# Split copies, half-batch loads and new ranks in the written-out order of an attention and FFN kernel

## The chip, the cores and the metric

The kernel runs on one core of one Trainium2 chip. The metric is the device time of one execution in microseconds. PE is the tensor engine, DVE the vector engine, ACT the scalar engine, POOL the GpSimd engine, which also issues most loads, and SP the sync engine.

## What is computed

Eight batches of eight heads, 576 positions and 64 dimensions go through a windowed attention. Heads 0 to 3 see the last 32 positions; heads 4 to 7 see every fourth of the last 128. The result, as 4608 rows of 512, goes through a multiplicative feed-forward network (FFN) without activation functions.

```python
scores = scale * np.matmul(q, k.transpose(0, 1, 3, 2))
mask_plain = (rel >= 0) & (rel < window)                                   # heads 0..3
mask_dil = (rel >= 0) & (rel < window * dilation) & (rel % dilation == 0)  # heads 4..7
attn = softmax(np.where(mask, scores, -1e9))
x = (attn @ v).transpose(0, 2, 1, 3).reshape(B * S, H * D)                 # 4608 x 512
a = x @ w1                                                                 # 512 -> 1024
b = x @ w2
h = a * b @ w3
out = h @ w_out                                                            # 1024 -> 512
```

## The kernel before

The kernel never forms `h @ w3`: it multiplies w3 by w_out once (1024 x 512, tile `wf_sb`) and applies the product to the gate `a * b`.

**Attention of a batch.** Heads come in two halves, u = 0 and u = 1. Loads bring q, k and v rows in bf16 (`load_rows`, line 245; for the u = 0 half of q and k of batch 0, whole float rows by `load_whole`, line 254, rounded by ACT in `round_rows`, line 271). DVE turns them with 32x32 transposes (`turn`, lines 379 and 394; the tasks are named T). PE forms scores in groups of blocks of 96 queries (line 445; tasks S). Batch 0 has four groups of three blocks, and a bias matmul (line 428) puts the mask into PSUM. Later batches have groups of five, and DVE multiplies by a mask after the exp (line 464; tasks M). ACT takes the exp (line 456; tasks E). In batches 0 and 1 the values are turned too: PE transposes them back (`v_back`, line 403; VT), and a copy puts them from PSUM into tile `vp` (`v_keep`, lines 413 and 415; VK). From batch 2 on values are loaded in place. For each quarter of a batch, PE multiplies by the values (line 481; V), DVE takes the reciprocal of the sums (line 492; R) and scales (line 504; N). In batches 0 and 1 PE transposes the result (line 521; X), and a copy puts it into tile `XT` (`keep`, lines 529 and 531; K). Later batches use a DMA transpose.

A task's name carries its place: K0.2 is the copy of batch 0, third quarter, and VK0.1.1 the value copy of batch 0, u = 1, second half.

**The FFN.** A unit is 288 rows, two to a batch. For unit k and column block f, PE forms A{k}.{f} and B{k}.{f} with four matmuls each (`up`, line 553), ACT copies A (line 564), and DVE multiplies both into the gate ring `gt` (line 569). The two units of batch 0 come first, four column blocks at a time in turn. The first product needs the copies K0.0, K0.1 and K0.2, and columns 0 to 255 of w1 and w2. Every 128 rows, eight matmuls with `wf_sb` make a piece of the output (`down`, line 580), which ACT copies and SP stores. w3 comes in eight blocks of rows: PE transposes one (line 638; W3T), ACT copies it (line 645; W3C), PE multiplies it by w_out (line 650; W3M), and ACT or DVE rounds it into `wf_sb` (lines 661 and 663; W3D).

**The order.** Every engine executes its instructions in a written-out order. `Plan.run` makes it when the kernel is built, as a list scheduler: each task has an engine, a duration in ns, dependencies and a priority; whenever an engine is free, the ready task with the lowest priority value goes next. The eight PSUM banks are places that matmul tasks hold (`slot`); while the first FFN product hasn't begun and PE has nothing, fillers (line 692) are put in. The priorities come from `FIRST` for batch 0 and `RANK` for the later ones. `ON_DVE` names the copies that DVE makes and not ACT. FFN products have running numbers from 10 as priorities, W3M has 7, and S, V, VT and X have values of about -99 plus the batch. The loads form one queue on POOL. Their order is that of the calls of `load`: the u halves of batch 0, then `FIRST_LOADS`. In that tuple "30" is the first block of w3, "w0" columns 0 to 255 of w1 and w2 (two loads), "w1" the next 256 and "w2" the last 512, "o0" and "o1" the halves of w_out, and "q1", "k1", "v1" the rows of batch 1. In the model a load takes its issue time on POOL and then its transfer time on one DMA line that all share.

Of the kernel before, what the change touches and what calls it, by code (L numbers as in the profile page):

```python
# [32 lines left out]
DIRECT_V = 2  # L33
ORDER = (2, 3, 0, 1)
RES = (0, 2, 1, 3)
RANK = dict(E=0.4, VK=2, K=0.3, N=1.5, T=3, VT=0.3, S=0.4, V=0.05, X=0.2, W=6, C=-1)
FIRST = {"E": 2, "VK": 0.4, "K": 0.5, "N": 0.2, "T": 2, "VT": 0.05, "S": 0.2, "V": 0.05, "X": 0.4}
WARM = 14
FILL = 110
FIRST_LOADS = ("30", "31", "w0", "w1", "32", "w2", "o0", "o1", "q1", "k1", "33", "34", "v1", "35", "36", "37")  # L40
SHIFT = {}
ON_DVE = ("VK0.0.1", "VK1.0.1", "W3D1", "W3D3", "W3D7")
GRP = 5
WHOLE = ("qn", "kn")
BUSY = 4500
LEAD = 1.1

# [12 lines left out]
class Plan:  # L60
# [13 lines left out]
        return t  # L74

    def run(self):
        fills = []
        users = {id(t): [] for t in self.tasks}
        takers = {id(t): [] for t in self.tasks}
        left = {}  # L80
# [38 lines left out]
        while len(order) < n:  # L119
            progress = True  # L120
            while progress:
                progress = False
                for e in engines:
                    if free[e] > now:
                        continue
                    for r, t in sorted(waiting[e], key=lambda x: x[1].prio):
                        if r > now:
                            continue
                        at = place(t) if t.slot else 0
                        if at is not None:  # L130
# [12 lines left out]
                    waiting[e].remove((r, t))  # L143
                    t.start = now
                    if e == "DMA":
                        free[e] = now + t.dur[0]
                        if t.dur[1]:
                            dma = max(dma, now + t.dur[0]) + t.dur[1]
                            t.end = dma + 1900
                        else:  # L150
                            t.end = free[e]
                    else:
                        t.end = free[e] = now + t.dur
                        if e == "SP" and t.name[0] == "X" and dma > now:
                            t.end = free[e] = now + t.dur + BUSY
                            dma += 1.5 * t.dur
                    if t.slot:
                        t.place = at
                        held[at : at + t.slot] = [t] * t.slot
                        if t.slot == 4:  # L160
                            kept = None
                    order.append(t)
                    for u in users[id(t)]:
                        left[id(u)] -= 1
                        if not left[id(u)]:
                            r = max(d.end + (0 if d.eng == u.eng else d.lat) for d in u.deps)
                            waiting[u.eng].append((r, u))
                    progress = True
# [11 lines left out]
def kernel(  # L180
# [46 lines left out]
    kts = [const.tile([P, 2, PADK + S, 2], BF16, name=f"kt{i}") for i in range(2)]  # L227
    qts = [const.tile([P, 2, S, 2], BF16, name=f"qt{i}") for i in range(2)]
    vts = [const.tile([P, 2, PADK + S, 2], BF16, name=f"vt{i}") for i in range(1)]
    warm = const.tile([P, 512], BF16, name="warm")  # L230

    def bank(n, dtype=F32):
        at = ps[:, plan.now.place or 0, :]
# [118 lines left out]
    def no_halo():  # L352
        nc.vector.memset(bias[0:32, 0:5:4, :], -BIG)

    def masks_of_bias():

        for at, first, n in ((0, 0, 4), (4, 1, 2), (6, 4, 3), (9, 4, 3), (12, 0, 4)):
            nc.gpsimd.tensor_scalar(
                out=mask[:, at : at + n, :],
                in0=bias[:, first : first + n, :],  # L360
                scalar1=0.0,
                scalar2=None,
                op0=AL.is_ge,
            )

# [39 lines left out]
                )  # L405
        spread[(b, u, half)] = x

    def v_keep(b, u, half, eng):
        dst = vps[b % 2][:, 4 * u : 4 * u + 4, 3 * half : 3 * half + 3, 0:D]
        o = dst.rearrange("p h m (j c) -> p m h j c", c=2)  # L410
        i = spread[(b, u, half)].rearrange("p m c (h j) -> p m h j c", h=4)
        if eng == "ACT":
            nc.scalar.copy(out=o, in_=i)
        else:
            nc.vector.tensor_copy(out=o, in_=i)
# [50 lines left out]
    class Step:  # L466
# [57 lines left out]
                    identity=ident[0:QB, 0:QB],  # L524
                )

        def keep(self, eng):
            if eng == "ACT":
                nc.scalar.copy(out=self.cols(), in_=self.x)
            else:  # L530
                nc.vector.tensor_copy(out=self.cols(), in_=self.x)

        def back_dma(self):
            nc.sync.dma_start_transpose(
# [12 lines left out]
            return XT[0][:, b * BLK : (b + 1) * BLK, c, 48 * hf : 48 * hf + 48]  # L547
        return XT[1][:, k, c - 2, :].rearrange("p (r m t) -> p m r t", r=2, m=BLK)

    def up(k, f, w_sb, key):  # L550
        o = bank(UNIT)
        for j, c in enumerate(ORDER):
            nc.tensor.matmul(  # L553
                out=o,
                lhsT=w_sb[:, c, f * P : (f + 1) * P],
                rhs=unit_cols(k, c),
                start=(j == 0),
                stop=(j == DCH - 1),
            )
        held[(key, k, f)] = o  # L560

    def copy_a(k, f):
        a_sb = wk_pool.tile([P, UNIT], BF16, tag="asb", bufs=6, name="asb")
# [106 lines left out]
        return (RANK if b else FIRST)[kind]  # L670

    def warm_up():
        o = bank(512)
        for i in range(WARM):
            nc.tensor.matmul(out=o, lhsT=warm[:, 0:P], rhs=warm, start=True, stop=True)

# [12 lines left out]
            nc.vector.memset(t[0:32, :, 0, 0:D], 0.0)  # L689

    def fill():
        nc.tensor.matmul(out=bank(256), lhsT=warm[:, 0:P], rhs=warm[:, 0:256], start=True, stop=True)  # L692

    plan.fill, plan.fill_from = fill, 2000

    c1 = add("const", "DVE", 1200, [], first_constants, -99)
    c0 = add("const2", "DVE", 1400, [c1], constants, -98)
    add("warm", "PE", 700 + 427 * WARM, [c1], warm_up, 0)

    lw3, lwo = {}, {}  # L700
    dma_n = [0]
# [41 lines left out]
            for half in range(2)  # L743
        ]
    plan.dma = 1200 + 1350 * len(WHOLE)
    for u in range(2):
        for nm in ("qn", "kn", "vn"):
            if u or nm not in WHOLE:
                loads_rows(nm, 0, (u,))
    idt = add("ident", "DMA", (600, 0), [], lambda: make_identity(nc, ident), 2.5, lat=150)  # L750
    bnd = add("band", "DMA", (800, 0), [c1], band, 1.5, lat=150)
    blk = add("blocks", "ACT", 1200, [bnd], blocks, -5, lat=100)
    blk = add("no halo", "DVE", 150, [blk], no_halo, 0, lat=80)
    mk = add("masks", "DMA", (2500, 0), [blk], masks_of_bias, 26.5, lat=150)
    lw12 = {}
    for x in FIRST_LOADS:
        c = int(x[1])
# [6 lines left out]
        elif x[0] == "v" and DIRECT_V <= c:  # L764
            loads_v(c)
        else:
            loads_rows(x[0] + "n", c)

    FUSED, w3m = [], []
    for ft in sorted(lw3):  # L770
# [10 lines left out]
        FUSED.append(add(name, eng, dur, [z], lambda f=ft, e=eng: w3_done(f, e), -1, lat=100))  # L781

    kept, paced = {}, []
    prev = {"x": [None] * 4}
    readers, grp_of, todo, n_grp, steps = {}, {}, [], 0, 0

    def turns(b, u, nm, pr):
# [22 lines left out]
    for b in range(B):  # L810
# [9 lines left out]
        for u in range(2):  # L820
# [3 lines left out]
            for half in range(2):  # L824
# [3 lines left out]
                if (b, u, half) == (0, 1, 1):  # L828
                    late.append(x)
                name = f"VK{b}.{u}.{half}"  # L830
                eng, dur = ("DVE", 980) if name in ON_DVE else ("ACT", 880)
                vals[(b, u, half)] = [
                    add(name, eng, dur, [x, c0], lambda b=b, u=u, h=half, e=eng: v_keep(b, u, h, e),
                        10 * b + rank("VK", b), lat=100)
                ]
        if b >= DIRECT_V:
            hal = add(f"HALO{b}", "DVE", 820, LV[b] + [c0], lambda b=b: halo_v(b), 10 * b + 2,
# [6 lines left out]
        def group(blocks, biased):  # L844
# [11 lines left out]
            else:  # L856
# [2 lines left out]
                e = add("E" + n, "ACT", 160 + 330 * g.n, [s], g.exps, 10 * b + rank("E", b), lat=100,  # L859
                        after=old)  # L860
                ms = [
                    add(f"M{n}.{h}", "DVE", 150 + 100 * g.n, [e, mk], lambda h=h: g.masks(h),
                        10 * b + 2, lat=80)
                    for h in range(2)
                ]
# [19 lines left out]
        while steps < 4 * B:  # L885
# [18 lines left out]
            rc = add(f"R{n}", "DVE", 240, [vv], st.recip, 10 * bb + rank("N", bb), lat=0,  # L904
                     after=[prev["x"][i]])
            ns = [
                add(f"N{n}", "DVE", 960 if u == 0 else 555, [vv, rc],
                    lambda st=st, part=part: st.norm(part), 10 * bb + rank("N", bb), lat=80)
# [2 lines left out]
            if bb < TURNED:  # L911
                x = add("X" + n, "PE", 310, ns + [idt], st.back, bb - 99 + rank("X", bb), slot=1)
                name = f"K{n}"
                eng, dur = ("DVE", 460) if name in ON_DVE else ("ACT", 640)
                x = add(name, eng, dur, [x], lambda st=st, eng=eng: st.keep(eng),
                        10 * bb + rank("K", bb), lat=100)
            else:
                x = add("XD" + n, "SP", 1300, ns, st.back_dma, 0, lat=1200)
            kept.setdefault(bb, []).append(x)
            prev["x"][i] = x  # L920
            vdone.setdefault(bb, []).append(vv)

    seq = 10
    G, Y, gates, stores, pairs = {}, {}, [], [], []

    def ups(k, f):
        nonlocal seq
        b, hf = k // 2, k % 2
        need = kept[b][0:2] + kept[b][2 + hf : 3 + hf]
# [3 lines left out]
        seq += 1  # L933
        a = add(f"A{k}.{f}", "PE", 490, need + wl, lambda: up(k, f, w1_sb, "a"), seq, slot=1,
                after=free + pairs[-1:])
        pairs.append(a)
        ca = add("CA", "ACT", 400, [a], lambda: copy_a(k, f), -1, lat=100,
                 after=[gates[-6] if len(gates) > 5 else None])
        seq += 1
        bb = add(f"B{k}.{f}", "PE", 490, need + wl, lambda: up(k, f, w2_sb, "b"), seq,  # L940
                 slot=1, after=[a])
        G[(k, f)] = add("G", "DVE", 460, [bb, ca], lambda: gate(k, f), -1, lat=100)
        gates.append(G[(k, f)])

    def downs(i):
# [71 lines left out]
```

## Time and profile before

| | before |
|---|---|
| time, three runs | 255.77, 255.88, 255.93 us |
| time of the profiled execution | 255.86 us |
| its span from first to last instruction | 254.1 us |
| PE, DVE, ACT, POOL busy | 246.2, 165.6, 125.9, 66.3 us |
| granted PE clock, mean | 1.000 |
| FFN products (L553) | 1024 matmuls, 136.2 us busy |
| second FFN step (L580) | 280 matmuls, 65.8 us busy |
| w3 times w_out (L650) | 64 matmuls, 14.8 us busy |
| fillers (L692) | 37 matmuls, 4.9 us busy |

PE's busy time counts a matmul from its start to its end, and matmuls overlap, so 0.286 us for a matmul of L553 is more than its share of the stream: in the chain of waits four of them take 0.49 us. Busy time of fillers is in the sum too.

Loads land in the order of issue, each some 6 to 19 us after it was issued:

| load | issued, us | landed, us |
|---|---|---|
| last half of v of batch 0 | 4.46 | 11.9 |
| w3 block 0 | 5.00 | 13.1 |
| w0, second of two | 6.8 | 17.3 |
| w1, second of two | 9.38 | 19.8 |
| w2, second of two | 13.37 | 26.4 |
| w_out, second half | 16.01 | 31.5 |
| q and k of batch 1 | 17.65, 18.77 | 35.0, 37.5 |
| v of batch 1 | 24.15 | 42.7 |
| w3 block 7 | 32.03 | 46.4 |

### The profile page before, as it was taken

What the parts mean: (1) busy time and instruction counts of PE and PEld (TensorE: products, weight loads), DVE (VectorE), ACT (ScalarE), POOL (GpSimd) and SP (SyncE); (2) the same over time, 40 slices, a digit from 0 to 9 for tenths busy, and PEclk for the clock granted to TensorE, in tenths of its full rate; (3) what the DMA queues carried; (4) which work ended last, traced back from release to release, by engine and by line L of the source; (5) the groups of instructions that cost most, each with busy time, mean ns of one, the idle gap of its engine ahead of it and who ended that gap; (6) DMA issues with size and microseconds to landing.
All of it is one profiled execution on the core that took longest, in us unless ns stands there. A gap on an engine that the chain in (4) does not pass through costs nothing.

```text
span 254.1 us, 6809 instructions
## 1 busy us (share of the span) xinstructions
PE 246.2 (97%) x2763; PEld 170.0 (67%) x2763; DVE 165.6 (65%) x342; ACT 125.9 (50%) x221; POOL 66.3 (26%) x103
## 2 busy tenths in 40 slices
PE   7699999999999999999999999999999999999994
PEld 3488766565777666667676766776767666777662
DVE  3983447799889898678767886837737365333321
ACT  5677333986635534463636626355353553333331
POOL 7653129643622712008260310700000000000000
PEclk9999999999999999999999999999999999999999
DMA  7999999999999999828999758852332223311114
GB/s 226 206 198 206 207 212 210 208 102 180 193 148 172 205 187 172 190 67 140 166 144 149 105 69 109 121 100 67 65 67 67 66 68 67 101 33 56 42 41 124
DMA packets 59374, 33.40 MB, mean 131 GB/s; under 512 B 44752, under 2 KB 49232, under 8 KB 59344
## 3 DMA queue, kind: packets, MB, share of 16 engines
q0 software_dynamic: 38544, 18.81, 58.0%
q1 hardware_dynamic: 20656, 14.10, 24.8%
q8 instruction: 21, 0.34, 0.6%
q14 instruction: 9, 0.07, 0.1%
q10 hardware_dynamic: 144, 0.07, 0.1%
HBM read 38.80 MB, written 9.44 MB: 190 GB/s over the span
## 4 chain that ended last, share of the span: by engine, by line
PE 93%; ACT 3%; DMA 2%; DVE 1%; issue 0%; ACTq 0%
PE ps L553 50%; PE ps L580 24%; PE ps L650 5%; PE ps L481 4%; PE ps L445 4%; DMA gt<-in_q_dram 2%; ACT et L456 2%; PE ps L692 2%; PE ps L638 1%; PE ps L403 1%; PE ps L521 1%; ACT w3T L645 1%; PE ps L598 1%; DVE qt L394 1%; ACT qn L271 0%; DVE kt L379 0%
## 5 line engine op out<-in xcount | busy, mean ns | idle before, releaser
L553 PE MATMUL ps<-XT,w_sb 128*128 128x288 bf16 x1024 | 136.2, 286 | 0.0
L553 PEld LDWEIGHTS <-w_sb 128*128 128x128 bf16 x1024 | 97.8, 98 | 30.6
L569 DVE TENSOR_TENSOR gt<-ps,asb 128x288 bf16<-128x288 f32 x128 | 57.7, 455 | 51.9 <-PE ps L553 49.6
L564 ACT CAST asb<-ps 128x288 bf16<-128x288 f32 x128 | 50.8, 398 | 51.9 <-PE ps L553 49.6
L580 PE MATMUL ps<-wf_sb,gt 128*128 128x512 bf16 x280 | 65.8, 379 | 0.0
L591 ACT COPY osb<-ps 128x512 f32<-128x512 f32 x35 | 20.5, 585 | 56.4 <-PE ps L580 54.6
L580 PEld LDWEIGHTS <-gt 128*128 128x128 bf16 x280 | 27.4, 98 | 26.9
L293 POOL DMA_DIRECT2D vp<-in_v_dram x48 | 29.9, 630 | 40.7 <-PE ps L481 18.5
L456 ACT ACTIVATE et<-ps 128x1920 bf16<-128x1920 f32 (+2 forms) x21 | 34.2, 1633 | 5.5 <-PE ps L445 4.8
L504 DVE TENSOR_TENSOR xo<-ps,rcp 96x384 bf16<-96x384 f32 (+1 forms) x48 | 31.5, 676 | 0.6
L464 DVE TENSOR_TENSOR et<-et,mask 128x960 bf16<-128x960 bf16 (+1 forms) x34 | 21.4, 645 | 4.9 <-ACT et L456 4.7
L394 DVE STREAM_TRANSPOSE qt<-qn 128x320 uint32<-128x320 uint32 (+3 forms) x34 | 22.4, 669 | 2.1 <-ACT qn L271 1.9
L481 PEld LDWEIGHTS <-et 128*128 128x128 bf16 x384 | 14.3, 98 | 1.7
L481 PE MATMUL ps<-vp,et 128*128 128x65 bf16 x384 | 15.1, 193 | 0.0
L650 PE MATMUL ps<-wo_sb,w3T 128*128 128x512 bf16 x64 | 14.8, 379 | 0.1
L394 DVE STREAM_TRANSPOSE kt<-kn 128x320 uint32<-128x320 uint32 (+3 forms) x18 | 11.6, 644 | 4.4 <-PE ps L445 4.3
L445 PE MATMUL ps<-qt,kt 32*128 32x96 bf16 x768 | 12.1, 201 | 1.9 <-DVE kt L379 1.9
L445 PEld LDWEIGHTS <-kt 32*128 32x128 bf16 x768 | 9.1, 92 | 7.0 <-issue 4.5
L492 DVE RECIPROCAL rcp<-ps 96x12 f32<-96x12 f32 x32 | 6.8, 216 | 10.6 <-PE ps L481 10.3
L245 POOL DMA_DIRECT2D kn<-in_k_dram x8 | 5.5, 685 | 27.9 <-DVE kt L394 16.2
L379 DVE STREAM_TRANSPOSE kt<-kn 128x576 uint32<-128x576 uint32 (+1 forms) x9 | 9.9, 1121 | 1.4 <-PE ps L445 1.4
L650 PEld LDWEIGHTS <-w3T 128*128 128x128 bf16 x64 | 5.9, 98 | 6.8 <-ACT w3T L645 0.6
(55 smaller groups left out, 118.2 us busy)
## 6 DMA issues: line engine op xcount, KB each, us to landing
qn<-in_q_dram POOLq DMA_DIRECT2D x7, 576.0 KB, 8.1
kn<-in_k_dram POOLq DMA_DIRECT2D x7, 576.0 KB, 7.4
w3n<-in_moe_w_dram POOLq DMA_DIRECT2D x8, 256.0 KB, 15.2
out_dram<-osb SPq DMA_DIRECT2D x7, 256.0 KB, 2.5
out_dram<-osb SPq DMA_DIRECT2D x8, 224.0 KB, 3.0
vp<-in_v_dram POOLq DMA_DIRECT2D x6, 288.0 KB, 10.3
out_dram<-osb SPq DMA_DIRECT2D x8, 192.0 KB, 2.9
out_dram<-osb SPq DMA_DIRECT2D x8, 160.0 KB, 3.9
```

Of the source, the lines that this page charges most:

```text
L293: nc.gpsimd.dma_start(out=vp[32 + p0 : 32 + p0 + n, 4:8, m, 0:D], in_=v_rows(b, 4, 4 * t0 + res, [[4 * D, n], [S * D, 4], [1, D]]),)
L394: nc.vector.transpose(out=o, in_=i)
L445: nc.tensor.matmul(out=self.sp[:, g, QB * i : QB * i + QB], lhsT=kt[prt, u, QB * m : QB * m + P, c], rhs=qq, start=(c == 0 and not biased) ...
L456: nc.scalar.activation(out=ev, in_=self.sp[:, :, 0:x], func=ACT.Exp, scale=scale)
L464: nc.vector.tensor_tensor(out=ev, in0=ev, in1=mk, op=AL.mult)
L481: nc.tensor.matmul(out=self.o[:, g, mm, :], lhsT=grp.et[:, c0 : c0 + P], rhs=vps[self.b % 2][:, 4 * self.u + g, 3 * self.hf + mm, 0 : D + ...
L504: nc.vector.tensor_tensor(out=dst, in0=self.o[0:QB, hs, :, 0:D], in1=self.rcp[0:QB, hs, :].unsqueeze(3).to_broadcast([QB, n, 3, D]), op=AL ...
L553: nc.tensor.matmul(out=o, lhsT=w_sb[:, c, f * P : (f + 1) * P], rhs=unit_cols(k, c), start=(j == 0), stop=(j == DCH - 1),)
L564: nc.scalar.copy(out=a_sb, in_=held[("a", k, f)])
L569: nc.vector.tensor_tensor(out=gt[:, f, c0 : c0 + UNIT].rearrange("p (r m t) -> p m r t", r=2, m=BLK), in0=held[("b", k, f)].rearrange("p ( ...
L580: nc.tensor.matmul(out=y, lhsT=gt[:, f, c0 : c0 + P], rhs=wf_sb[:, f, :], start=(f == 0), stop=(f == KFF - 1),)
L650: nc.tensor.matmul(out=o, lhsT=w3T[ft][:, g, :], rhs=wo_sb[:, g, :], start=(g == 0), stop=(g == KFF - 1),)
```

## The change

The diff does these things.

- A copy named in `HALVED` becomes two tasks, one on ACT and one on DVE, each for half of the columns (K) or of the heads (VK). `ON_DVE` changes: DVE makes all of K0.2 and VK0.1.1, and ACT all of VK0.0.1. Three of the w3 roundings stay on DVE, but others.
- q, k and v of batch 1 are loaded as six loads of one u half each, and `FIRST_LOADS` puts them among the weights: the first half of v after w0, the first halves of k and q after w3 block 1.
- `Plan.run` keeps the landing times of loads and lets a load issue only when the one eight before it has landed.
- The masks of the later batches are made by five tasks instead of one, at priority 19.5 and up instead of 26.5.
- The warm-up has 25 matmuls of 256 columns for 14 of 512, and its tile half the columns.
- All priorities in `RANK` and `FIRST` change, and the FFN products number from 20.
- `up` can be split into two tasks, but with `PARTED = 0` no product is.

```diff
-RANK = dict(E=0.4, VK=2, K=0.3, N=1.5, T=3, VT=0.3, S=0.4, V=0.05, X=0.2, W=6, C=-1)
-FIRST = {"E": 2, "VK": 0.4, "K": 0.5, "N": 0.2, "T": 2, "VT": 0.05, "S": 0.2, "V": 0.05, "X": 0.4}
-WARM = 14
+RANK = dict(E=0.5, VK=3, K=2, N=0.2, T=0.5, VT=0.05, S=0.1, V=0.05, X=0.1, W=0.5, C=5)
+FIRST = {"E": 3, "VK": 1, "K": 0.2, "N": 2, "T": 0.2, "VT": 0.05, "S": 0.3, "V": 0.1, "X": 0.3}
+WARM = 25
-FIRST_LOADS = ("30", "31", "w0", "w1", "32", "w2", "o0", "o1", "q1", "k1", "33", "34", "v1", "35", "36", "37")
+FIRST_LOADS = ("30", "w0", "v10", "w1", "w2", "31", "k10", "q10", "o0", "o1", "32", "33", "34", "q11", "k11", "v11", "35", "36", "37")
-ON_DVE = ("VK0.0.1", "VK1.0.1", "W3D1", "W3D3", "W3D7")
+ON_DVE = ("K0.2", "VK0.1.1", "W3D1", "W3D4", "W3D5")
+B0_LOADS = ("v0", "q1", "k1", "v1")
+HALVED = ("K0.0", "K0.1", "K0.3", "K1.1", "VK0.0.0", "VK0.1.0", "VK1.0.1", "VK1.1.0")
+MASK_AT = 19.5
+PARTED = 0
...
                         if t.dur[1]:
-                            dma = max(dma, now + t.dur[0]) + t.dur[1]
+                            if len(landed) >= 8:
+                                free[e] = max(now, landed[-8]) + t.dur[0]
+                            dma = max(dma, free[e]) + t.dur[1]
                             t.end = dma + 1900
+                            landed.append(t.end)
...
-    warm = const.tile([P, 512], BF16, name="warm")
+    warm = const.tile([P, 256], BF16, name="warm")
...
-    mk = add("masks", "DMA", (2500, 0), [blk], masks_of_bias, 26.5, lat=150)
+    mk = [
+        add(f"masks{i}", "DMA", (x, 0), [blk], lambda i=i: mask_of_bias(i), MASK_AT + 0.1 * i,
+            lat=150)
+        for i, x in enumerate((1200, 710, 940, 940, 1200))
+    ]
...
-            loads_rows(x[0] + "n", c)
+            loads_rows(x[0] + "n", c, (int(x[2]),) if x[2:] else None)
...
                 eng, dur = ("DVE", 980) if name in ON_DVE else ("ACT", 880)
+                ways = [(eng, dur, slice(0, 4))]
+                if name in HALVED:
+                    ways = [("ACT", 540, slice(0, 2)), ("DVE", 560, slice(2, 4))]
...
                 eng, dur = ("DVE", 460) if name in ON_DVE else ("ACT", 640)
+                ways = [(eng, dur, slice(0, 6 * QB))]
+                if name in HALVED:
+                    ways = [("ACT", 400, slice(0, 3 * QB)), ("DVE", 270, slice(3 * QB, 6 * QB))]
...
-    seq = 10
+    seq, parted = 20, 0
```

More of the change, by code (lines that the diff above doesn't have):

```diff
@@ L76, in run @@
     def run(self):
-        fills = []
+        fills, landed = [], []
         users = {id(t): [] for t in self.tasks}
@@ L353, in no_halo, with mask_of_bias @@
         nc.vector.memset(bias[0:32, 0:5:4, :], -BIG)
[L355 to L364, printed above, removed]
+    MASKS = ((0, 0, 4), (4, 1, 2), (6, 4, 3), (9, 4, 3), (12, 0, 4))
+    def mask_of_bias(i):
+        at, first, n = MASKS[i]
+        nc.gpsimd.tensor_scalar(
+            out=mask[:, at : at + n, :],
+            in0=bias[:, first : first + n, :],
+            scalar1=0.0,
+            scalar2=None,
+            op0=AL.is_ge,
+        )
     def turn(b, u, nm, part):
@@ L406, in v_back, with v_keep @@
         spread[(b, u, half)] = x
-    def v_keep(b, u, half, eng):
+    def v_keep(b, u, half, eng, hs=slice(0, 4)):
         dst = vps[b % 2][:, 4 * u : 4 * u + 4, 3 * half : 3 * half + 3, 0:D]
-        o = dst.rearrange("p h m (j c) -> p m h j c", c=2)
-        i = spread[(b, u, half)].rearrange("p m c (h j) -> p m h j c", h=4)
+        o = dst.rearrange("p h m (j c) -> p m h j c", c=2)[:, :, hs, :, :]
+        i = spread[(b, u, half)].rearrange("p m c (h j) -> p m h j c", h=4)[:, :, hs, :, :]
         if eng == "ACT":
@@ L525, in back, with keep @@
                 )
-        def keep(self, eng):
+        def keep(self, eng, c=slice(0, 6 * QB)):
             if eng == "ACT":
-                nc.scalar.copy(out=self.cols(), in_=self.x)
+                nc.scalar.copy(out=self.cols()[:, c], in_=self.x[:, c])
             else:
-                nc.vector.tensor_copy(out=self.cols(), in_=self.x)
+                nc.vector.tensor_copy(out=self.cols()[:, c], in_=self.x[:, c])
         def back_dma(self):
@@ L548, in unit_cols, with up @@
         return XT[1][:, k, c - 2, :].rearrange("p (r m t) -> p m r t", r=2, m=BLK)
-    def up(k, f, w_sb, key):
-        o = bank(UNIT)
-        for j, c in enumerate(ORDER):
+    def up(k, f, key, chunks=ORDER, first=True, last=True):
+        if first:
+            held[(key, k, f)] = bank(UNIT)
+        for j, c in enumerate(chunks):
             nc.tensor.matmul(
-                out=o,
-                lhsT=w_sb[:, c, f * P : (f + 1) * P],
+                out=held[(key, k, f)],
+                lhsT={"a": w1_sb, "b": w2_sb}[key][:, c, f * P : (f + 1) * P],
                 rhs=unit_cols(k, c),
-                start=(j == 0),
-                stop=(j == DCH - 1),
+                start=(first and j == 0),
+                stop=(last and j == len(chunks) - 1),
             )
-        held[(key, k, f)] = o
     def copy_a(k, f):
@@ L672, in warm_up @@
     def warm_up():
-        o = bank(512)
+        o = bank(256)
         for i in range(WARM):
@@ L691, in fill @@
     def fill():
-        nc.tensor.matmul(out=bank(256), lhsT=warm[:, 0:P], rhs=warm[:, 0:256], start=True, stop=True)
+        nc.tensor.matmul(out=bank(256), lhsT=warm[:, 0:P], rhs=warm, start=True, stop=True)
     plan.fill, plan.fill_from = fill, 2000
@@ L697 @@
     c0 = add("const2", "DVE", 1400, [c1], constants, -98)
-    add("warm", "PE", 700 + 427 * WARM, [c1], warm_up, 0)
+    add("warm", "PE", 700 + 213 * WARM, [c1], warm_up, 0)
     lw3, lwo = {}, {}
@@ L745 @@
     plan.dma = 1200 + 1350 * len(WHOLE)
[L746 to L749, printed above, removed]
+    for x in B0_LOADS:
+        loads_rows(x[0] + "n", 0, (int(x[1]),))
     idt = add("ident", "DMA", (600, 0), [], lambda: make_identity(nc, ident), 2.5, lat=150)
@@ L783 @@
     kept, paced = {}, []
-    prev = {"x": [None] * 4}
+    prev = {"x": [[]] * 4}
     readers, grp_of, todo, n_grp, steps = {}, {}, [], 0, 0
@@ L831 @@
                 eng, dur = ("DVE", 980) if name in ON_DVE else ("ACT", 880)
+                ways = [(eng, dur, slice(0, 4))]
+                if name in HALVED:
+                    ways = [("ACT", 540, slice(0, 2)), ("DVE", 560, slice(2, 4))]
                 vals[(b, u, half)] = [
-                    add(name, eng, dur, [x, c0], lambda b=b, u=u, h=half, e=eng: v_keep(b, u, h, e),
+                    add(name, e, dur, [x, c0],
+                        lambda b=b, u=u, h=half, e=e, hs=hs: v_keep(b, u, h, e, hs),
                         10 * b + rank("VK", b), lat=100)
+                    for e, dur, hs in ways
                 ]
@@ L861, in group @@
                 ms = [
-                    add(f"M{n}.{h}", "DVE", 150 + 100 * g.n, [e, mk], lambda h=h: g.masks(h),
+                    add(f"M{n}.{h}", "DVE", 150 + 100 * g.n, [e] + mk, lambda h=h: g.masks(h),
                         10 * b + 2, lat=80)
@@ L904 @@
             rc = add(f"R{n}", "DVE", 240, [vv], st.recip, 10 * bb + rank("N", bb), lat=0,
-                     after=[prev["x"][i]])
+                     after=prev["x"][i])
             ns = [
@@ L914 @@
                 eng, dur = ("DVE", 460) if name in ON_DVE else ("ACT", 640)
-                x = add(name, eng, dur, [x], lambda st=st, eng=eng: st.keep(eng),
+                ways = [(eng, dur, slice(0, 6 * QB))]
+                if name in HALVED:
+                    ways = [("ACT", 400, slice(0, 3 * QB)), ("DVE", 270, slice(3 * QB, 6 * QB))]
+                x = [
+                    add(name, e, dur, [x], lambda st=st, e=e, c=c: st.keep(e, c),
                         10 * bb + rank("K", bb), lat=100)
+                    for e, dur, c in ways
+                ]
             else:
-                x = add("XD" + n, "SP", 1300, ns, st.back_dma, 0, lat=1200)
+                x = [add("XD" + n, "SP", 1300, ns, st.back_dma, 0, lat=1200)]
             kept.setdefault(bb, []).append(x)
@@ L928, in ups @@
         b, hf = k // 2, k % 2
-        need = kept[b][0:2] + kept[b][2 + hf : 3 + hf]
+        plain = kept[b][0] + kept[b][1]
+        need = plain + kept[b][2 + hf]
         wl = lw12[(0, 0, 1, 1, 2, 2, 2, 2)[f]]
@@ L932, in ups, with product @@
         free = [Y[i] for i in range(max(0, lap // P), (lap + UNIT - 1) // P + 1)]
-        seq += 1
-        a = add(f"A{k}.{f}", "PE", 490, need + wl, lambda: up(k, f, w1_sb, "a"), seq, slot=1,
-                after=free + pairs[-1:])
+        def product(key, after):
+            nonlocal seq, parted
+            name = f"{key.upper()}{k}.{f}"
+            seq += 1
+            if k or parted == PARTED:
+                return add(name, "PE", 490, need + wl, lambda: up(k, f, key), seq, slot=1,
+                           after=after), []
+            parted += 1
+            p = add(name + "p", "PE", 245, plain + wl,
+                    lambda: up(k, f, key, ORDER[2:], last=False), seq - 5, slot=1, after=after)
+            return add(name, "PE", 245, need + [p],
+                       lambda: up(k, f, key, ORDER[:2], first=False), seq), [p]
+        a, p = product("a", free + pairs[-1:])
         pairs.append(a)
-        ca = add("CA", "ACT", 400, [a], lambda: copy_a(k, f), -1, lat=100,
+        ca = add("CA", "ACT", 400, [a] + p, lambda: copy_a(k, f), -1, lat=100,
                  after=[gates[-6] if len(gates) > 5 else None])
[L939 to L942, printed above, removed]
+        bb, p = product("b", p or [a])
+        bb = [bb] + p
+        G[(k, f)] = add("G", "DVE", 460, bb + [ca], lambda: gate(k, f), -1, lat=100)
         gates.append(G[(k, f)])
```

## The prediction

> **What bounds the kernel now.** I read the table of busy time by stretch first, with cuts where the chain of waits changes character. The columns are length, then busy time and count for PE, PEld, DVE, ACT and POOL, then granted clock, DMA share and GB/s.
>
> ```profile
> core 0: us, PE busy (x) PEld busy (x) DVE busy (x) ACT busy (x) POOL busy (x), PEclk, DMA share, GB/s
> 8.79:21.73 12.94, 12.29 (x252) 10.52 (x253) 9.53 (x22) 10.05 (x12) 6.55 (x10) 1.00 1.27 204
> 21.73:41.33 19.60, 19.60 (x152) 14.00 (x151) 9.81 (x21) 7.52 (x17) 6.48 (x10) 1.00 1.17 208
> 41.33:59.32 17.99, 17.84 (x256) 11.78 (x255) 15.96 (x27) 15.05 (x19) 9.73 (x14) 1.00 1.24 162
> 80.00:245.00 165.00, 165.00 (x1779) 114.47 (x1778) 105.81 (x216) 75.09 (x143) 28.29 (x41) 1.00 0.69 106
> ```
>
> PE is full from 21.73 us to the end. Nothing done to another engine there can save time unless a PE gap goes. So I looked for PE time that isn't work. The chain of waits (start, length, what) shows it before 21.73, and once more near 45:
>
> ```profile
> 8.79 0.47 PE ps L445 x24
> ...
> 16.30 1.64 PE ps L692 x15
> 17.94 0.49 PE ps L428 x4
> ...
> 19.50 1.64 PE ps L692 x15
> 21.14 0.36 PE ps L481 x12
> 21.51 0.22 PE ps L692 x2
> 21.73 1.47 PE ps L553 x12
> ...
> 43.77 1.01 ACT w3T L645
> 44.78 1.67 ACT et L456
> 46.46 0.91 ACT w3T L645
> 47.42 1.90 PE ps L650 x8
> ```
>
> L692 is the filler matmul; its busy time is no work. From 8.79 to 21.73 the real work at the chain's own spacings is 8.21 us: scores 1.64 (L445), bias 1.47 (L428), value transposes 1.76 (L403), two w3 transposes 0.90 (L638), three output transposes 0.98 (L521), values 1.46 (L481). So 12.94 - 8.21 = 4.73 us are fillers and waits. In 41.33 to 59.32 it is 17.25: L553 1.96, five L650 groups at 1.727 = 8.63, five w3 transposes 2.26, scores 1.10, value transposes 1.36, values 1.10, output transposes 0.84. So 0.74 us are stall, around PE's waits for the ACT copies of L645. These 5.5 us are all that a new order can gain.
>
> What holds the first FFN product (L553, called A0.0) at 21.5 is in the timeline of ACT and of DVE:
>
> ```profile
> 18.85 1.13 ACT L456 ACTIVATE et<-ps 128x1152 bf16<-128x1152 f32 x1 [0.78 <-PE ps L445]
> 19.88 0.79 ACT L413 COPY vp<-ps 128x768 bf16<-128x768 bf16 x1
> 20.56 0.66 ACT L529 COPY XT<-ps 128x576 bf16<-128x576 bf16 x1
> 17.64 0.91 DVE L394 STREAM_TRANSPOSE vt<-vn 128x160 uint32<-128x160 uint32 x2
> 21.62 0.23 DVE L492 RECIPROCAL rcp<-ps 96x12 f32<-96x12 f32 x1 [3.07 <-PE ps L481]
> ```
>
> The copy K0.2 (L529 at 20.56) is the last input of A0.0. Its transpose was done at 19.5; it stood behind an exp and a value copy on ACT, while DVE was idle for 3.07 us.
>
> [...]
>
> **The change part by part.**
>
> *Warm-up and its memset.* 25 x 256 columns for 14 x 512. [...] Nothing follows: scores wait for DVE's L379 until 8.79. The memset halves (-0.14 of 0.27), DVE idling before 6.19. Zero.
>
> *Halved copies.* [...] In batch 0 ACT loses five halves (K0.0, K0.1, K0.3, VK0.0.0, VK0.1.0) and two wholes (K0.2, VK0.1.1) to DVE and takes over one whole (VK0.0.1). In batch 1 three more are halved, off the path.
>
> *New ranks.* The decisive edit. For batch 0, turns (T) go to 0.2 and norms (N) to 2 on DVE, so all turns and value copies come ahead of the norms. Following the planner's rule by hand, DVE's queue from the turn of v at 8.57 is, with spacings of the trace: turn of v 1.08, four of q 1.51, two of k 0.75, half VK 0.50, six turns 2.22, R 0.20, half VK 0.50, VK0.1.1 0.87, R 0.20, N 0.88, R 0.20, N 0.88, half K 0.28, half N 0.51, half K 0.28, half N 0.51. Sum 11.37, so N0.2 ends at 19.94. Then transpose X0.2 to 20.4, K0.2 on DVE to 20.85, A0.0 at 20.95. That is 0.78 ahead of 21.73. DVE is never idle there, so ACT's relief doesn't help more.
> But PE then has more left. V0.3 (0.37) isn't done, since its exp ends about 20.9. The second w3 block comes later (next part), so its transpose (0.45) moves from filler time into the full stretch. 0.82 lost against 0.78 won: **front +0.04**.
>
> *Load order.* The same bytes in three more issues on POOL's queue (about 0.55 each, hidden: a load is issued some 10 us before it lands). Landings are 1.25 us apart for 256 KB, so by the new order: w0 at 15.7 (17.3 before), w1 19.7, w2 24.9, second w3 block 26.2, k and q of batch 1, first half, 29.0, o1 34.0 (31.5 before), last w3 block about 46 (46.4). A0.0 needs w0 by 20.95, later columns w1 by 22.9 and w2 by 29: no wait. o1 is needed by the first W3M, after 15.7 us of FFN products and some 3 us of batch 1: about 39. No wait.
> Masks go as five instructions (4.76 us, seen at 38.75) to after the nineteenth load, about 22.5 to 27.5. Six loads queue behind them, but those already in flight reach to 36.5, so the DMA engines don't run dry.
>
> *Batch 1 in halves.* The first half of its turns, exp, masks, norm and value copies can go into 21.7 to 39, where DVE is busy 9.81 of 19.60 and ACT 7.52, out of 41 to 59, where they are at 15.96 and 15.05 of 17.99. By then five w3 blocks have landed, so copies of L645 run ahead of the products. I take the 0.74 us of stall as gone: **-0.74**. Bounds: all kept and 0.9 added, or all gone.
>
> *The load limit, `up` with parts, product numbers from 20.* PARTED is 0, so no product is split; these only order. Zero.
>
> Sum 0.04 - 0.74 = -0.70 us. The profiled execution spans 254.1 with a time of 255.86; the runs are 255.77 to 255.93. I put the difference on 255.88: **255.2 us**.
>
> **Rivals.**
>
> *More is gained (254.1).* A norm slips in wherever a turn waits for its landing (v at 11.9, k at 10.4), and N0.2 ends about 1.1 us sooner. For it: those landings are close to the queue's times. Against: by my sum DVE reaches each turn after its data. -0.70 - 1.1 = -1.8.
>
> *The front's gain is given back (255.9).* PE stalls as before in 41 to 59, since ACT's exp of 1.77 still stands before a copy of L645. Then +0.04.
>
> *ACT becomes the bound near 50 us (256.9).* The copies of L645 now rank after K and value halves of batch 0 and no longer first. The last three blocks land together with batch 1's second half (q, k, v 39 to 42). If its exp (1.77) goes ahead of the first of those copies (1.02), W3M waits 2.8 while PE has only 12 value transposes (0.69) and three w3 transposes (1.35): 0.8 stall. The value half on ACT then waits for three copies, 3.05, and PE runs out of L650 before K1.2: 0.8 more. It decides once the exp is queued first. 1.6 for 0.74, and 0.04: +0.9 to +1.1. For it: ACT is 84% busy there already. Against: K1.2 came at 58.8 without a PE gap.
>
> *The change does not do what it says:* a split copy's second half is late on a full DVE, so A0.0 doesn't move. Then the front is +0.8, inside the last case.
>
> **How the numbers follow.** Likeliest 0.36 (254.5 to 255.5), more gained 0.16, given back 0.17, ACT bound 0.31. A measurement here tells 0.2% (0.51 us) from none. Faster: 0.30 + 0.16 + 0.04 = 0.50. Same: 0.06 + 0.11 + 0.03 = 0.20. Slower: 0.02 + 0.28 = 0.30. The range takes most of the second and of the last case: 253.9 to 257.0.
>
> **What would show it.** L553 should start near 20.9 with K0.2 on DVE just before; N after all L394 of batch 0; a w3 transpose inside the full stretch; L692 under 37; batch 1's first exp with masks before 41; no PE wait for L645 at 43 to 51. A start of L553 after 21.7, or ACT in the chain between 45 and 60 by over 1 us, makes it wrong.

## The result, and the profile after

| | before | changed |
|---|---|---|
| time, median of four runs | 255.86 us (255.77 to 255.93) | 254.97 us (254.89 to 255.04) |
| span of the profiled execution | 254.1 us | 253.2 us |
| fillers | 37 | 23 |

The ratio is 0.9965, with a 95% interval of 0.9948 to 0.9982. The changed kernel is 0.89 us faster, where 0.7 was forecast. The two parts of the forecast sum were both wrong, and this is what the rest is about.

In the changed kernel line numbers are higher by some 10. L563 is the FFN product (553 before), L701 the filler (692), L659 W3M (650), L647 W3T (638), L538 and L540 the copies K on ACT and DVE, L424 the value copy VK on DVE, L513 the norms (504).

Below is the table of busy time by stretch of the changed kernel, cut about where the first FFN product, the first W3M and the third unit start. Columns are as in the prediction.

```profile
8.73:20.27 11.54, 10.06 (x222) 7.96 (x223) 10.99 (x27) 7.58 (x10) 5.33 (x8) 1.00 1.28 202
20.27:38.25 17.98, 17.88 (x196) 14.28 (x194) 11.74 (x24) 10.08 (x21) 10.15 (x15) 1.00 1.18 209
38.25:58.36 20.11, 20.03 (x220) 12.08 (x220) 15.83 (x29) 12.69 (x17) 8.45 (x14) 1.00 1.24 170
```

The front is shorter, with DVE busy 10.99 of 11.54 us: it has become the bound there, as forecast. PE is nearly full afterwards, as before. Batch 1's first half did move forward, but DVE still works 15.83 of 20.11 us in the third stretch.

The chain of waits of the changed kernel (start, length, what):

```profile
15.73 2.60 DVE xo L513 x4
18.33 0.23 DVE XT L540
...
19.04 0.71 PE ps L701 x5
19.74 0.37 PE ps L490 x12
20.11 0.33 PE ps L701 x3
20.44 1.47 PE ps L563 x12
...
29.21 0.45 PE ps L647 x8
...
50.40 1.22 DVE et L473 x2
```

Before, the chain had 16.30 to 21.73 filled with 3.5 us of L692. Now the four norm instructions of three quarters run back to back on DVE, N0.2 is over at 18.33, and the first product stands at 20.44 for 21.73. K0.2 itself ends at 20.0; V0.3 and three fillers, which the written order puts in front of the product, hold PE until 20.44. The transpose of the second w3 block sits at 29.21, inside the full stretch.

**Where the 0.89 us come from.** The third unit can only start when batch 1's attention and all of w3 are done, so its start sums up the first two stretches. In the chain it is at 59.32 before and at 58.36 after, -0.96. From there to the end neither profile shows a wait of PE. So:

- First product sooner: 21.73 to 20.44, **-1.29**.
- Work left over from the front: only W3T1, the transpose of the second w3 block, **+0.45**. V0.3 is done (19.74), as it was before.
- PE time without work between the first product and the third unit. Before, at the chain's own spacings, the work is X0.3 0.26, six W3T 2.70, 128 matmuls of products 15.68, eight W3M 13.82, scores 1.10, value transposes 1.36, values 1.10 and X of batch 1 0.84. That is 36.86 of 37.59, which leaves 0.73. After, it is 36.86 + 0.45 of 37.92, which leaves 0.61: **-0.12**.

### The profile page after: what moved, and what is told of

It reads as the page before. It is cut to its first block, busy times and chain, and to the rows that moved or that the text cites. A ratio compares the mean times of both kernels' runs of the same rounds, so it can differ in the third digit from the quotient of the medians.

```text
span 253.2 us, 6818 instructions
## 1 busy us (share of the span) xinstructions
PE 245.8 (97%) x2760; PEld 170.6 (67%) x2760; DVE 167.9 (66%) x350; ACT 124.3 (49%) x221; POOL 67.8 (27%) x106
## 3 DMA queue, kind: packets, MB, share of 16 engines
q0 software_dynamic: 38592, 18.81, 58.7%
## 4 chain that ended last, share of the span: by engine, by line
PE 90%; DVE 5%; DMA 2%; issue 1%; ACT 1%; ACTq 0%; DVEq 0%
PE ps L563 49%; PE ps L589 24%; PE ps L659 6%; PE ps L490 4%; PE ps L454 4%; DMA gt<-in_q_dram 2%; DVE qt L403 1%; DVE xo L513 1%; PE ps L647 1%; PE ps L607 1%; PE ps L701 1%; PE ps L530 1%; ACT qn L278 0%; DVE et L473 0%; PE ps L412 0%
## 5 line engine op out<-in xcount | busy, mean ns | idle before, releaser
L563 PE MATMUL ps<-XT,w_sb 128*128 128x288 bf16 x1024 | 136.3, 286 | 0.0
L563 PEld LDWEIGHTS <-w_sb 128*128 128x128 bf16 x1024 | 97.8, 98 | 30.6
L300 POOL DMA_DIRECT2D vp<-in_v_dram x48 | 30.3, 639 | 48.3 <-PE ps L490 30.3
L513 DVE TENSOR_TENSOR xo<-ps,rcp 96x384 bf16<-96x384 f32 (+1 forms) x48 | 31.4, 675 | 0.5
L473 DVE TENSOR_TENSOR et<-et,mask 128x960 bf16<-128x960 bf16 (+1 forms) x34 | 21.2, 645 | 6.8 <-ACT et L465 6.7
L490 PEld LDWEIGHTS <-et 128*128 128x128 bf16 x384 | 14.6, 98 | 1.9 <-issue 0.4
L490 PE MATMUL ps<-vp,et 128*128 128x65 bf16 x384 | 15.5, 193 | 0.1
L659 PE MATMUL ps<-wo_sb,w3T 128*128 128x512 bf16 x64 | 15.0, 379 | 0.1
L286 POOL DMA_DIRECT2D vp<-in_v_dram x6 | 7.2, 1194 | 11.5 <-PE ps L490 10.7
L659 PEld LDWEIGHTS <-w3T 128*128 128x128 bf16 x64 | 5.9, 98 | 6.3 <-issue 0.3
```

Of the source, the lines that this page charges most:

```text
L300: nc.gpsimd.dma_start(out=vp[32 + p0 : 32 + p0 + n, 4:8, m, 0:D], in_=v_rows(b, 4, 4 * t0 + res, [[4 * D, n], [S * D, 4], [1, D]]),)
L473: nc.vector.tensor_tensor(out=ev, in0=ev, in1=mk, op=AL.mult)
L490: nc.tensor.matmul(out=self.o[:, g, mm, :], lhsT=grp.et[:, c0 : c0 + P], rhs=vps[self.b % 2][:, 4 * self.u + g, 3 * self.hf + mm, 0 : D + ...
L513: nc.vector.tensor_tensor(out=dst, in0=self.o[0:QB, hs, :, 0:D], in1=self.rcp[0:QB, hs, :].unsqueeze(3).to_broadcast([QB, n, 3, D]), op=AL ...
L563: nc.tensor.matmul(out=held[(key, k, f)], lhsT={"a": w1_sb, "b": w2_sb}[key][:, c, f * P : (f + 1) * P], rhs=unit_cols(k, c), start=(first ...
L659: nc.tensor.matmul(out=o, lhsT=w3T[ft][:, g, :], rhs=wo_sb[:, g, :], start=(g == 0), stop=(g == KFF - 1),)
```

## The experiments

Theory F says that PE is full from the first product to the end, so the time moves by the start of that product, plus the work left undone in front of it, plus what stalls arise later. Theory S is the prediction's: the gain sits in the second stretch, in batch 1's halves.

**e1. The kernel before, and K0.2 alone moved to DVE.**

```diff
-ON_DVE = ("VK0.0.1", "VK1.0.1", "W3D1", "W3D3", "W3D7")
+ON_DVE = ("K0.2", "VK0.0.1", "VK1.0.1", "W3D1", "W3D3", "W3D7")
```

> The kernel before with one edit: the copy K0.2 on VectorE. Theory F (PE is full from the first FFN product to the end, so the time moves by the start of that product less the work left undone): K0.2 starts as soon as its transpose ends, the first L553 about 1.2 us sooner, V0.3 (0.37 us) then falls into the full stretch; about 255.1 us. Theory S (the gain sits in the second stretch, in batch 1's halves): 255.9 us, no change.

Measured: 254.88 us for 255.83, ratio 0.9964 (0.9955 to 0.9973). One name in a tuple brings what the whole change brings. One line of its timeline on DVE, and its chain:

```profile
19.59 0.46 DVE L531 COPY XT<-ps 128x576 bf16<-128x576 bf16 x1 [1.05 <-PE ps L521]
```

```profile
19.48 0.77 PE ps L692 x7
20.25 0.99 PE ps L553 x8
21.24 0.37 PE ps L481 x12
...
58.29 0.49 PE ps L553 x4
```

The copy starts 0.1 us after its transpose, on a DVE that was idle, and the product is 1.48 us sooner. V0.3 (L481, 0.37) falls behind it. The third unit is at 58.29, 1.03 us sooner. So a gain of this size needs nothing of theory S: the loads, masks and ranks here are those of before.

**e2. The changed kernel without halves, all copies on their former engines.**

```diff
-ON_DVE = ("K0.2", "VK0.1.1", "W3D1", "W3D4", "W3D5")
-HALVED = ("K0.0", "K0.1", "K0.3", "K1.1", "VK0.0.0", "VK0.1.0", "VK1.0.1", "VK1.1.0")
+ON_DVE = ("VK0.0.1", "VK1.0.1", "W3D1", "W3D3", "W3D7")
+HALVED = ()
```

> The changed kernel with no copy halved and the copies on their former engines; new ranks and load order kept. Theory F: the first L563 starts about 0.6 us later than in the changed kernel, the rest as there; 255.4 to 255.7 us. Theory S: as the changed kernel, 255.0 us.

Measured: 254.62 us, ratio 0.9953 (0.9937 to 0.9970). Theory F's number is missed, and theory S's 255.0 is nearer: this kernel isn't slower than the changed one, and the two intervals overlap. The split copies of the title aren't needed for the gain once the ranks and the loads are new. What was wrong in theory F's number is my estimate of the start; e8 shows it.

**e3. The changed kernel with batch 1 loaded whole and late.**

```diff
-FIRST_LOADS = ("30", "w0", "v10", "w1", "w2", "31", "k10", "q10", "o0", "o1", "32", "33", "34", "q11", "k11", "v11", "35", "36", "37")
+FIRST_LOADS = ("30", "w0", "w1", "w2", "31", "o0", "o1", "q1", "k1", "32", "33", "34", "v1", "35", "36", "37")
```

> The changed kernel with batch 1 loaded whole and after the weights, in the place it had before; the front's order is kept. Theory F: the first L563 at 20.3 as in the changed kernel and the gain kept, 254.9 to 255.3 us. Theory S: the gain is lost, 255.7 us or more, with PE gaps between 41 and 60 us.

Measured: 256.39 us, ratio 1.0018 (1.0011 to 1.0026): slower than before, 1.4 us over the changed kernel. The front is the same (first product at 20.40). PE's timeline shows the loss:

```profile
40.80 0.33 PE L647 MATMUL ps<-ident,w3n 128*128 128x128 bf16 x3
42.49 0.62 PE L454 MATMUL ps<-qt,kt 32*128 32x96 bf16 x40 [1.36 <-DVE kt L388]
```

PE has run through its products and waits 1.36 us for the turned k of batch 1. The load is not what comes last: by the chain of waits the turn of k follows DVE's turn of q (40.80) and no transfer. In the written order it stands, at 41.21, behind a w3 rounding, for which DVE idles 2.74 us until 37.83, and three turns of q. Later, at 93.25, PE waits another 0.51 us. So theory S has a true core that it put the wrong way round: the early half loads don't recover the stall of before, they prevent a new one, which this order has when the first product comes sooner. e1 shows that not every order has it.

**e4. The changed kernel with the second w3 block loaded right after the first.**

```diff
-FIRST_LOADS = ("30", "w0", "v10", "w1", "w2", "31", "k10", ...
+FIRST_LOADS = ("30", "31", "w0", "v10", "w1", "w2", "k10", ...
```

> The changed kernel with the second w3 block loaded right after the first, so that its eight transposes (0.45 us) fall in front of the first FFN product. Theory F: they are taken from filler time, 0.45 us less than the changed kernel, 254.5 us. Theory S: no change, 255.0 us.

Measured: 254.44 us, ratio 0.9939 (0.9925 to 0.9952); 0.53 us below the changed kernel. Its chain:

```profile
18.81 0.45 PE ps L647 x8
...
20.33 1.47 PE ps L563 x12
...
57.80 1.96 PE ps L563 x16
```

The transpose lies at 18.81, in filler time, and the third unit starts 0.56 us sooner than in the changed kernel. This is the 0.45 that the new load order gave away, measured with a start 0.11 sooner. w0 stands one block later in the queue without harm: the product is at 20.33 for 20.44.

**e5. The changed kernel with K0.2 on ACT.**

```diff
-ON_DVE = ("K0.2", "VK0.1.1", "W3D1", "W3D4", "W3D5")
+ON_DVE = ("VK0.1.1", "W3D1", "W3D4", "W3D5")
```

> The changed kernel with the one copy K0.2 back on ScalarE. If the move of K0.2 alone makes the gain in this order too, as it did in the kernel before: about 0.7 us is lost, 255.6 to 255.9 us. If it only matters where ScalarE is full just then (in the new order ScalarE idles from 19.3 to 21.0 us): 254.8 to 255.1 us, as the changed kernel.

Measured: 254.77 us, ratio 0.9949 (0.9935 to 0.9963): as the changed kernel. The reason is in ACT's timeline of the changed kernel:

```profile
17.42 1.13 ACT L465 ACTIVATE et<-ps 128x1152 bf16<-128x1152 f32 x1 [1.62 <-DVE xo L513]
18.59 0.70 ACT L538 COPY XT<-ps 128x288 bf16<-128x288 bf16 x2
```

After 19.29 ACT is free until 20.96. The profiled execution of e5 itself took 1.6 us more than the median, and its norms start 1.63 us later than in the changed kernel (17.36 for 15.73). Counted from the first norm, its product comes no later than in the changed kernel, 4.49 us after it for 4.71:

```profile
17.36 2.60 DVE xo L513 x4
...
21.85 0.98 PE ps L563 x8
```

K0.2 on DVE is worth 0.95 us where ACT was full with an exp and a value copy (e1), and nothing here. The two ways to a sooner product don't add.

**e6. The kernel before with only the halves of batch 0.**

```diff
+HALVED = ("K0.0", "K0.1", "K0.3", "VK0.0.0", "VK0.1.0")
...
+                if name in HALVED:
+                    ways = [("ACT", 540, slice(0, 2)), ("DVE", 560, slice(2, 4))]
...
+                if name in HALVED:
+                    ways = [("ACT", 400, slice(0, 3 * QB)), ("DVE", 270, slice(3 * QB, 6 * QB))]
```

> The kernel before with only the five halved copies of batch 0; ranks, loads, masks, warm-up and K0.2 on ScalarE as before. If the halves make the gain: 255.0 us. Theory F: K0.2 still waits for the value copy on ScalarE, and the third group of scores is ordered later, so the first L563 is not sooner and may be 0.5 us later: 255.8 to 256.5 us.

Measured: 258.02 us, ratio 1.0084 (1.0065 to 1.0103): 2.1 us slower. The sign was right, the size was four times too small. In the trace the first product is at 23.86, and DVE's timeline shows why:

```profile
11.36 0.44 DVE L403 STREAM_TRANSPOSE kt<-kn 128x160 uint32<-128x160 uint32 x1
11.66 1.39 DVE L424 COPY vp<-ps 128x384 bf16<-128x384 bf16 x2
...
16.67 0.41 DVE L403 STREAM_TRANSPOSE kt<-kn 128x128 uint32<-128x128 uint32 x1
```

With the old ranks a half value copy slips in between the two turns of k that the third score group needs, and a whole value copy, two norms and a half K follow it; the second turn is at 16.67, where the kernel before had both turns done at 12.07. (The profiled execution was 1.3 us over the median. In it the granted clock was 0.50 from 11.79 to 14.16 us, eight fillers ahead of the values taking 1.71 us, and PE waited 1.28 us for an exp at 67.5. Which of these delays the median run has can't be told from it.)

**e7. e4 without any halves; K0.2 and VK0.1.1 stay on DVE.**

```diff
-HALVED = ("K0.0", "K0.1", "K0.3", "K1.1", "VK0.0.0", "VK0.1.0", "VK1.0.1", "VK1.1.0")
+HALVED = ()
```

> As e4 (second w3 block right after the first), and no copy halved; K0.2 and VK0.1.1 stay on VectorE. Theory F: in this order V0.3 and the w3 transpose come ahead of the first product, which starts up to 0.5 us sooner than in e4: 253.9 to 254.3 us. If the halves carry part of the gain: 254.6 us or more.

Measured: 253.85 us for 255.89, ratio 0.9918 (0.9903 to 0.9933). This beats both kernels: 2.0 us below the kernel before. In e4's order the halves cost 0.59 us. Its chain:

```profile
18.07 0.37 PE ps L490 x12
18.43 0.45 PE ps L647 x8
18.88 0.26 PE ps L530 x6
19.14 0.45 PE ps L647 x8
19.59 0.44 PE ps L701 x4
20.02 0.49 PE ps L563 x4
...
57.27 1.47 PE ps L563 x12
```

V0.3 (L490), both w3 transposes and X0.2 are all done before the product at 20.02, with four fillers left. Against e4 the start is 0.31 sooner and the third unit 0.53.

**e8. e2 with the second w3 block early.** The edit of e4 on e2.

> As e2 (no halves, copies on their former engines), and the second w3 block right after the first. Theory F: e2's 254.6 less the w3 transpose of 0.45 us, 254.2 us. If e2's time was chance and not its order: 254.7 us or more.

Measured: 254.30 us, ratio 0.9933 (0.9919 to 0.9946). e2's time wasn't chance. The chain has the product at 20.38, for 20.33 in e4, so my "0.6 us later" for the old copies was wrong: with the new ranks ACT had room for whole copies.

```profile
20.38 0.49 PE ps L563 x4
...
57.62 0.98 PE ps L563 x8
```

**e9. e7 with batch 1 loaded whole and late.**

```diff
-FIRST_LOADS = ("30", "31", "w0", "v10", "w1", "w2", "k10", "q10", "o0", "o1", "32", "33", "34", "q11", "k11", "v11", "35", "36", "37")
+FIRST_LOADS = ("30", "31", "w0", "w1", "w2", "o0", "o1", "q1", "k1", "32", "33", "34", "v1", "35", "36", "37")
```

> As e7 (no halves, second w3 block early: the best so far, 253.85 us), but with batch 1 loaded whole and after w_out, in the place it had before. If the early loads are needed once the first product starts sooner: PE waits for the first scores of batch 1 as in e3 (1.36 us there), 254.9 to 255.6 us. If e3's loss belonged to its halved copies: 253.9 us, as e7.

Measured: 258.33 us (256.95 to 258.61), ratio 1.0083 (1.0062 to 1.0105), 4.5 us above e7. The direction was right, the size wasn't. PE's timeline of the run with 256.95 us:

```profile
39.18 0.61 PE L647 MATMUL ps<-ident,w3n 128*128 128x128 bf16 x8
42.40 0.62 PE L454 MATMUL ps<-qt,kt 32*128 32x96 bf16 x40 [2.60 <-DVE kt L388]
```

PE waits 2.60 us where e3 waited 1.36. e3's loss didn't belong to its halved copies. One other run took 256.96 us; the remaining four are 1.2 to 1.7 us longer, with a mean granted clock of 0.990 to 0.993 for 1.000, and why no profile shows. By the two short runs the loss is 3.1 us.

**e10. The changed kernel with the masks at their old place in POOL's queue.**

```diff
-MASK_AT = 19.5
+MASK_AT = 26.5
```

> The changed kernel with the masks back at their old place, after the loads of batch 2's q and k (about 40 us and not 24 us). The mask tasks are costed at nothing in the prediction. If that holds: 255.0 us. If the early first group of batch 1 needs them: its mask multiplication waits until about 44 us and PE behind it, 256 to 258 us.

Measured: 256.62 us, ratio 1.0024 (1.0014 to 1.0034), 1.65 us above the changed kernel. The masks run from 37.0 to 41.7 for 24.0 to 28.7, and the first mask multiplication (L473) is at 44.35 for 38.01. It waits for its place in the written-out order rather than for the masks, since the planner put it after their modelled end. V1.0 falls to 50.92, for 39.97 in the changed kernel, among the rest of batch 1. Later products wait for what follows: PE stands still for 0.55 us before 88.01 and for 0.80 us before 95.37. (The profiled execution is the slowest of ten, 0.5 us over the median.)

**e11. e4 with the batch 0 ranks of the kernel before.**

```diff
-FIRST = {"E": 3, "VK": 1, "K": 0.2, "N": 2, "T": 0.2, "VT": 0.05, "S": 0.3, "V": 0.1, "X": 0.3}
+FIRST = {"E": 2, "VK": 0.4, "K": 0.5, "N": 0.2, "T": 2, "VT": 0.05, "S": 0.2, "V": 0.05, "X": 0.4}
```

> As e4 (halves kept, second w3 block early), with the batch 0 ranks of the kernel before: norms ahead of turns, so the first product starts about 1.2 us sooner, but one value transpose (0.22), V0.3 (0.37) and the fourth quarter's work are then left to the full stretch. Theory F: the start less the work left gives 253.8 to 254.4 us. If the new ranks carry the gain: 255 us or more.

Measured: 255.75 us, ratio 0.9992 (0.9980 to 1.0004): all of e4's gain is gone, and F's number was missed by over a microsecond. The chain:

```profile
19.96 0.60 PE ps L563 x4
20.56 0.34 PE ps L412 x6
...
22.54 0.37 PE ps L490 x12
22.91 2.45 PE ps L563 x20
25.36 0.27 PE ps L530 x6
25.65 0.41 ACT XT L538
...
26.09 0.32 DVE XT L540
...
26.44 9.84 PE ps L563 x79
```

The product starts 0.37 us sooner than in e4 (not 1.2), but leaves a value transpose (0.34) and V0.3 (0.37), so it's behind by 0.34. Then the fourth quarter is so late that PE waits for both halves of K0.3, from 25.63 to 26.44: 0.81. Together 1.15 of the 1.30 by which the third unit (59.10 for 57.80) is later. The early product was bought with the second unit's input, and the new `FIRST` is worth 1.3 us in e4's order.

**The account over the runs.** Starts in the chain, and what the third unit's start says against the measured time:

| kernel | first product | third unit | third unit, to before | time, to before |
|---|---|---|---|---|
| before | 21.73 | 59.32 | | |
| changed | 20.44 | 58.36 | -0.96 | -0.89 |
| e1 | 20.25 | 58.29 | -1.03 | -0.95 |
| e4 | 20.33 | 57.80 | -1.52 | -1.39 |
| e7 | 20.02 | 57.27 | -2.05 | -2.04 |
| e8 | 20.38 | 57.62 | -1.70 | -1.59 |
| e11 | 19.96 | 59.10 | -0.22 | -0.08 |

These are the kernels whose profiled execution lies within 0.05 us of the median. In them the third unit's start predicts each time to within 0.14 us. The first product's start doesn't: e11 has the earliest and hardly a gain. It isn't enough where stalls come later still, as in e3 and e10.

## Why the prediction was right, and where its working was wrong

**The time and the direction** held: 255.2 for 254.97, within 253.9 to 257.0, faster. The sum 0.04 - 0.74 came out as -0.84 - 0.12. The errors nearly cancelled. That the time came out so close is luck, and no proof of the working. The signs that it had named came too (the norms behind all turns, 23 fillers, a mask multiplication at 38.01, no wait of PE for L654 from 43 to 51 us), and didn't tell the right working from the wrong one.

**The step that failed: "all turns and value copies come ahead of the norms".** The turns did. VK0.1.1 did not, and I had put its 0.87 us ahead of the norms. DVE's timeline of the changed kernel:

```profile
14.29 0.94 DVE L403 STREAM_TRANSPOSE vt<-vn 128x160 uint32<-128x160 uint32 x2
...
15.65 2.68 DVE L513 TENSOR_TENSOR xo<-ps,rcp 96x768 bf16<-96x768 f32 x4
18.25 0.30 DVE L540 COPY XT<-ps 128x288 bf16<-128x288 bf16 x1
18.47 0.95 DVE L424 COPY vp<-ps 128x768 bf16<-128x768 bf16 x1
```

The value copy (18.47) is after the norms, and so are the half copies of K. PE's timeline gives the cause:

```profile
15.85 0.28 PE L437 MATMUL ps<-bias,ident 128*128 128x288 bf16 x1 [0.27 <-ACT w3T L654]
16.59 0.41 PE L437 MATMUL ps<-bias,ident 128*128 128x288 bf16 x2 [0.46 <-DVE xo L513]
```

The bias matmuls of the fourth score group stand at the head of PE's queue and wait 0.27 and 0.46 us for PSUM banks which a w3 copy and the norms hold. The value transposes (L412, 17.45) are queued behind them. The planner counts these places too: given sixteen instead of eight, it writes VK0.1.1 ahead of N0.1 and N0.2. I followed the engines' ranks by hand and not the places in PSUM. N0.2 ended at 18.33 and not 19.94; of the 1.61 us between, 0.87 are VK0.1.1 and 0.56 the two half copies of K that my sum had put in front of it. The rival that gained more had foreseen a sooner N0.2, by 1.1 us, but for another reason: it let a norm slip between turns.

**"V0.3 isn't done, since its exp ends about 20.9"** failed for the same reason: the exp ended at 18.55, and V0.3 ran at 19.58, before the product. That is the other 0.37 us.

**The 0.45 of W3T1** was right: in e4 the third unit starts 0.56 us sooner, and 0.11 of that is the sooner product.

**"I take the 0.74 us of stall as gone"** failed: 0.12 went. The waits around L645 were real and are gone, but PE got others nearly as long: it waits for ACT ahead of the first W3M (38.25), and at 50.40 the chain of the changed kernel passes through DVE's mask multiplications (L473), with the values and W3M behind them. Moving batch 1's first half forward relieved DVE and ACT in that stretch and bought, against the kernel before, 0.12 us at most.

**Costs.** Of the copies K and VK the profile before shows whole ones alone: K on ACT 0.658 us (median of L529), VK 0.944 on DVE (L415) and 0.806 on ACT (mean of L413). What the sum put in for half copies and for K0.2 on DVE, that profile doesn't show; it was my estimate. Measured in the changed kernel: K0.2 whole on DVE 0.45 us (0.46 in e1), half K 0.30 on DVE and 0.40 on ACT, half VK 0.55 on DVE and 0.48 on ACT. On DVE the sum was within 0.05 us of each.

**"Zero" for the masks** was right for the queue and too narrow as a claim: e10 shows that 1.65 us depend on their place, through the order that is planned around them. Likewise the loads: no PE wait for w0, w1, w2 or w_out was seen, as forecast, but the half loads were worth 1.4 us (e3), and 3.1 to 4.5 us in e7's order (e9), against a stall that the kernel before didn't have.

**The rival of a bound ACT** didn't come. The second exp of batch 1 did go ahead of three copies of L654 (51.12 to 53.98), but between 45 and 58 us ACT isn't in the chain; what PE waits for there is DVE.

**What the ranks did:** all of `RANK` is without effect: with the old `RANK` the planner writes the same order on every engine. What carries the change is what e2 keeps. Of that, `FIRST` (e11), the half loads (e3, e9) and the place of the masks (e10) each cost 1.3 us or more when taken back. The load limit, the warm-up and the numbers of the products weren't run by themselves, and `FIRST` wasn't run on the kernel before alone.

## What to carry to other kernels

Where one engine is full from some point on, count what is left for it at that point, and not only when it starts: a start that leaves work behind or starves the next unit gains nothing (e11), and work moved into its idle time gains its own length (e4). A copy moved to an idle engine is worth the queue that it leaves, so look who stands before it: 0.95 us in one order, none in another (e1, e5). When an order is made from a model, an edit moves instructions far from itself (e6, e10), so each part has to be tried in the order that it will live in.

## What the runs showed of the hardware

In the profiled execution of e6 the granted clock fell to half. By the table of stretches it was at 0.76 in 10 to 12 us and at 0.50 in 12 to 14:

```profile
10.00:12.00 2.00, 1.74 (x39) 1.57 (x39) 1.93 (x7) 1.64 (x2) 0.87 (x2) 0.76 1.11 209
12.00:14.00 2.00, 2.00 (x21) 1.62 (x19) 1.05 (x2) 0.48 (x1) 1.16 (x2) 0.50 1.18 201
```

A filler took 0.214 us there (eight in 1.71 us), for 0.109 in the kernel before (fifteen in 1.64 us). PE had idled 2.35 us before its first scores at 9.00; in the kernel before it idled 1.88 us in the same place, and the clock was 1.00 in every stretch from 1 to 16 us. What set off the fall in e6 these runs don't show.
